# Two weight matrices converted where they are used, a scratch tile of its own for the conversion, and the sink rows of v loaded earlier, in an attention and feed-forward kernel on one core

## The chip, the cores and the metric

The kernel runs on one core of a Trainium2 chip. The metric is the time of one execution on the device, in microseconds (us); it is the median of the runs of one kernel. Engines are called as in the profile: PE multiplies matrices, PEld loads its weights, DVE is the vector engine, ACT the scalar engine, POOL is GpSimd, and SP issues DMAs.

## The reference

Sliding-window attention with sink keys for 4 batches, 8 heads, 768 rows and head size 64 (window 128, 4 sinks), then a feed-forward block with a squared ReLU (model 512, inner 2048), then a second block with two inputs multiplied (inner 1024) on the 3072 tokens of 512:

```python
attn = softmax(mask(q @ k.T / 8)) @ v            # per batch and head
x = attn.transpose(0, 2, 1, 3).reshape(3072, 512)
h = np.maximum(x @ w_in, 0.0)                    # w_in 512 x 2048
x = h * h @ w_out                                # w_out 2048 x 512
a, b = x @ w1, x @ w2                            # 512 x 1024 each
out = (a * b @ w3) @ w_out2                      # 1024 x 1024, 1024 x 512
```

The inputs of the attention and the weights lie in DRAM as float64.

## The kernel before

**Numbers.** Every matrix product of the two blocks is made of three f16 products: high by high, high by low, low by high. A weight is therefore prepared in two steps. First the float64 piece (128 x 512 numbers, 512 KB, in a tile named raw) becomes float32: `f64_to_f32_up` (L82 to L103) has ACT read the upper words as floats into cvy (L88), has DVE shift and mask the bits that are still missing in two instructions on 16-bit halves (L93, L96), and has DVE put both together (L99). `conv` (L1036) calls it. The two DVE shifts write over the raw tile itself, but for the pieces of `conv_late`, which take a scratch tile, cvt, of their own (`two=True`). Then `split` (L799) has ACT write the f16 high half and DVE (POOL for half of w_in) the low half. Raw pieces have two buffers (tag raw64). cvy and cvt are two of many names that share one ring of eight slots, tag t2 (`T2B = 8`): r, sq, x1e, the sink rows of v (vsr, vb, vt), and cp, cq, cr, asb of the output stage.

**Stages.** In the prologue the first 16 of 96 attention units are computed, and 8 pieces of w_in and some of the next are prepared. Six passes n = 0 to 5 over 512 tokens each follow, of 16 steps j (128 of the 2048 inner columns). One step is `ffn_A` (12 matmuls into hps), `ffn_act1` to `ffn_act3` (r, its square, and that as high and low half g), `ffn_B` of the step before (12 matmuls into x1ps), and, in passes 0 to 4, one attention unit of the tokens of the next pass (sc, softmax, pt, y). In passes 0 to 4 ACT, DVE and PE run in the order in which the program is written (the class `InOrder`, whose line L290 nearly every instruction bears); elsewhere a scheduler orders them. Pass 5 has no attention unit. The fold then makes w34 = w3 times w_out2: for each of eight f, `fold_T` transposes a row block of w3 on PE (w3ps, then w3T in two halves), and `fold_M` multiplies (24 matmuls into w34ps). The output stage takes six blocks of 512 tokens, each in eight f: `ffn_C` (a and b from w12, in seven products cps), `ffn_D` (ops) and `ffn_out`.

**Where weights are prepared.** The list `pieces` sets the order; `w_load` and `w_conv` walk it. w_in and w_out: prologue and pass 0. `load_late` and `conv_late` (L1076 to L1091): the 16 pieces of w3 and the 8 of w_out2 are converted in passes 1 to 3, one every two steps, and written back to DRAM as float32 (w3_dr, wo2_dr). w12 (16 pieces of w1 and w2, each pair summed as `ffn_C` needs it, `conv_w12` L1233): two late in pass 3, six in pass 4, six in pass 5, two in the fold. In pass 5 `load_wo2` (L1171) reads w_out2 back from DRAM and `split_wo2` has POOL make its low halves; `load_w3` (L1183) reads w3 back, one f at a time, for the fold.

**Sink rows of v.** Four times (b = 0 to 3), at unit ub - 1, `vs_load` (L621) clears a tile vsr on POOL and issues six small DMAs on SP, and `vs_make` at once works on it (vb, vt, vs on DVE). For b = 2 this is in pass 1, for b = 3 in pass 2; SP issues its DMAs in one order, the transposing loads of the probabilities (pt<-ph) among them.

## Time and profile before

| what | value |
|---|---|
| median of 3 runs | 1140.44 us (1139.66 to 1143.43) |
| the profiled execution, own time | 1145.11 us |
| its span in the trace | 1143.2 us |
| mean granted clock of PE | 0.973 of full speed |
| PE busy | 1051.2 us (92%) |
| DVE busy | 765.9 us (67%) |
| ACT busy | 703.2 us (62%) |
| POOL busy | 59.3 us (5%) |
| prologue | 0 to 91.2 us |
| passes 0 to 5 | from 91.2, 215.4, 322.3, 429.1, 536.5, 637.6 us |
| last hps ends, then fold | 726 us |
| output stage | 778.2 to 1143.2 us |

The starts of the passes are the first matmuls into hps of each. The busy share of the whole span says little, since the stages have different limits; what is read below is each stretch by itself. "Idle" of an engine is the time before an instruction in which it did nothing, with the event that ended it. A row of the chain of work that ended last names what was being waited for at that time, followed back from the end.

### The profile page before, as it was taken

How to read it: one execution, taken by the hardware profiler on the slowest of the kernel's cores; microseconds unless marked ns; L12 is line 12 of the kernel's file. 1: busy time of each engine (PE TensorE's matmuls, PEld its weight loads, DVE VectorE, ACT ScalarE, POOL GpSimd, SP SyncE). 2: the span in 40 equal slices, each digit the busy share in tenths (PEclk: the TensorE clock that was granted, in tenths of full speed). 3: DMA queues.
4: the chain of work that ended last, by engine and by line, in shares of the span. 5: the costliest groups of instructions: out<-in, count | busy, mean ns of one | idle time of the engine just before them, and what ended most of it. 6: DMA issues, size and time to landing. Idle time of an engine off the chain costs nothing.

```text
span 1143.2 us, 20444 instructions
## 1 busy us (share of the span) xinstructions
PE 1051.2 (92%) x7146; PEld 632.9 (55%) x7146; DVE 765.9 (67%) x2284; ACT 703.2 (62%) x1832; POOL 59.3 (5%) x167
## 2 busy tenths in 40 slices
PE   6777889999899989998999989999999999999996
PEld 5663444555455535544454434456767676767774
DVE  8997889877688868867997555555363636353433
ACT  6975768877467647655776785555464545464432
POOL 2111102000000000000000110000000000000000
PEclk9977989999899989999999999999999999999999
DMA  8847688989698868897853222123020101010101
GB/s 188 159 120 175 156 188 184 180 197 181 128 207 174 166 141 190 168 177 143 167 129 98 79 86 79 57 74 111 1 74 1 74 1 38 1 38 1 37 1 40
DMA packets 271232, 126.05 MB, mean 110 GB/s; under 512 B 238224, under 2 KB 254608, under 8 KB 270480
## 3 DMA queue, kind: packets, MB, share of 16 engines
q1 hardware_dynamic: 270832, 124.13, 48.7%
q8 instruction: 58, 0.95, 0.4%
q14 instruction: 54, 0.44, 0.1%
q10 hardware_dynamic: 288, 0.52, 0.1%
HBM read 68.37 MB, written 17.83 MB: 75 GB/s over the span
## 4 chain that ended last, share of the span: by engine, by line
PE 58%; DVE 16%; DMA 12%; ACT 7%; issue 3%; SPq 2%; POOL 0%; DVEq 0%; ACTq 0%
PE cps L290 18%; PE hps L290 12%; PE x1ps L290 11%; PE ops L290 11%; DMA pt<-ph 3%; PE w34ps L290 3%; DMA raw<-in_moe_w_dram 2%; DMA raw<-in_moe_w_out_dram 2%; PE y L290 2%; DVE pr L290 2%; DMA raw<-in_moe_w_in_dram 2%; DVE raw L96 2%; DVE cvy L99 2%; PE sc L290 2%; DVE raw L93 1%
## 5 line engine op out<-in xcount | busy, mean ns | idle before, releaser
L290 PE MATMUL x1ps<-g,wo 128*128 128x512 f16 x1152 | 271.9, 385 | 9.4 <-DVE g L290 6.9
L290 PE MATMUL hps<-xT,wi 128*128 128x512 f16 x1152 | 270.4, 385 | 2.8 <-ACT r L290 2.8
L290 PE MATMUL cps<-x1T,w 128*128 128x256 f16 x2016 | 231.5, 273 | 7.3 <-DVE cq L290 4.6
L290 PEld LDWEIGHTS <-w 128*128 128x128 f16 x2016 | 197.1, 98 | 44.4 <-issue 9.2
L290 PEld LDWEIGHTS <-wo 128*128 128x128 f16 x1152 | 111.2, 99 | 134.2 <-issue 20.3
L290 PEld LDWEIGHTS <-wi 128*128 128x128 f16 x1152 | 115.1, 100 | 125.5 <-issue 11.3
L290 PE MATMUL ops<-w,h 128*128 128x512 f16 x576 | 133.5, 379 | 1.8 <-ACT h L290 1.8
L290 ACT ACTIVATE r<-hps 128x512 f32<-128x512 f32 x96 | 56.8, 592 | 99.9 <-PE hps L290 97.5
L290 ACT ACTIVATE cp<-cps 128x256 f32<-128x256 f32 x96 | 36.1, 376 | 131.3 <-PE cps L290 131.3
L290 ACT ACTIVATE pr<-pr,stt 128x264 f32<-128x264 f32 (+1 forms) x176 | 77.5, 483 | 61.6 <-DVE stt L290 60.6
L290 PEld LDWEIGHTS <-h 128*128 128x128 f16 x576 | 56.3, 98 | 58.1 <-ACT h L290 2.1
L290 DVE SCALAR_TENSOR_TENSOR asb<-cq,cps 128x256 f32<-128x256 f32 x48 | 20.2, 420 | 87.6 <-PE cps L290 87.6
L290 DVE TENSOR_TENSOR ph<-pr,ph 128x512 f16<-128x512 f32 (+2 forms) x148 | 58.3, 431 | 30.6 <-ACT ph L290 30.6
L290 DVE CUSTOM_DVE_ANT_0 pr<-sc,mask 128x264 f32<-128x264 f32 (+1 forms) x176 | 65.4, 402 | 4.6 <-PE sc L290 4.3
L290 PEld LDWEIGHTS <-pt 128*128 128x128 f16 x956 | 40.0, 99 | 47.7 <-issue 24.6
L290 PE MATMUL y<-vp,pt 128*128 128x65 f16 (+1 forms) x888 | 41.1, 195 | 24.4 <-DVE xn L290 20.2
L290 PE MATMUL sc<-kT,qT 128*128 128x128 f16 x592 | 48.9, 223 | 13.1 <-DVE stt L290 13.0
L93 DVE TENSOR_SCALAR raw<-raw 128x512 uint16<-128x512 uint16 x48 | 36.7, 764 | 36.1 <-DMA raw<-in_moe_w_dram 23.0
L290 PEld LDWEIGHTS <-qT 128*128 128x128 f16 x592 | 41.3, 99 | 32.9 <-issue 9.8
L290 ACT ACTIVATE ph<-pr 128x512 f16<-128x512 f32 (+2 forms) x148 | 55.7, 420 | 5.1 <-DMA pt<-ph 3.1
L290 ACT ACTIVATE g<-r 128x512 f16<-128x512 f32 x88 | 55.3, 628 | 2.4
L88 ACT ACTIVATE cvy<-raw 128x512 f32<-128x512 f32 x72 | 48.1, 668 | 10.5 <-DMA raw<-in_moe_w_out_dram 9.3
(194 smaller groups left out, 1507.2 us busy)
## 6 DMA issues: line engine op xcount, KB each, us to landing
raw<-in_moe_w_dram SPq DMA_DIRECT2D x32, 512.0 KB
raw<-in_moe_w_out_dram SPq DMA_DIRECT2D x24, 512.0 KB
raw<-in_moe_w_in_dram SPq DMA_DIRECT2D x16, 512.0 KB
raw<-in_k_dram SPq DMA_DIRECT2D x84, 64.0 KB
raw<-in_q_dram SPq DMA_DIRECT2D x84, 64.0 KB
raw<-in_v_dram SPq DMA_DIRECT2D x84, 64.0 KB
x_dr<-x1e SPq DMA_DIRECT2D x20, 256.0 KB
x1s<-x_dr SPq DMA_DIRECT2D x5, 1024.0 KB
```

The source lines that it names most:

```text
L88: nc.scalar.activation(out=y.bitcast(F32), in_=raw.bitcast(F32)[:, :, 1], func=ACTF.Abs, scale=2.0 ** -111, accum_out=stat)
L93: nc.vector.tensor_scalar(out=t2[:, :, 0], in0=half[:, :, 1], scalar1=13, scalar2=None, op0=ALU.logical_shift_right)
L96: nc.vector.tensor_scalar(out=t2[:, :, 1], in0=half[:, :, 3], scalar1=0x8000, scalar2=None, op0=ALU.bitwise_and)
L99: nc.vector.scalar_tensor_tensor(out=dst, in0=y, scalar=3, in1=t, op0=ALU.logical_shift_left, op1=ALU.bitwise_or)
L290: r = f(*args, **kw)
```

## The change

- `f64_to_f32_up` always gets a scratch tile: `conv` takes cvt from the ring t2 for every piece, and the raw tile is only read.
- w3_dr, wo2_dr, `load_late` and `conv_late` are gone. The 8 pieces of w_out2 are converted in pass 5 and split at once (low halves on DVE, no longer on POOL); the pieces of w3 are loaded and converted in the fold, and `fold_T` transposes from the converted tile. Of w3, even f go into a 1 MB tile in the place of the output tile ost, odd f into the two raw buffers.
- Pass 5 has a list of 16 items, one a step: w_out2 four, w12 two, w_out2 two, w12 two, w_out2 two, w12 four; then the loads of w3 f = 1.
- w12: one pair of pieces in each of passes 1 to 4, at j = 4 and 5, with the loads of the next ones behind the conversions; 8 pieces in pass 5; none in the fold.
- vsr has a tile of its own in the attention's pool, and `vs_load` is called at unit ub - 6 for b = 1 to 3; `vs_make` stays at ub - 1.
- `ffn_out` is called after the second part of `ffn_C` rather than ahead of it.

```diff
...
 UP_MOST = 2.0 ** 31
 
 
-def f64_to_f32_up(nc, raw, y, dst, stat, t=None):
-
-
-    own = t is None
-    t = raw[:, :, 0] if own else t
+def f64_to_f32_up(nc, raw, y, dst, stat, t):
+
+
     nc.scalar.activation(
         out=y.bitcast(F32), in_=raw.bitcast(F32)[:, :, 1], func=ACTF.Abs, scale=2.0 ** -111, accum_out=stat
     )
     half = raw.bitcast(U16)
-    t2 = half if own else t.bitcast(U16).rearrange("p (n c) -> p n c", c=2)
+    t2 = t.bitcast(U16).rearrange("p (n c) -> p n c", c=2)
     nc.vector.tensor_scalar(
         out=t2[:, :, 0], in0=half[:, :, 1], scalar1=13, scalar2=None, op0=ALU.logical_shift_right
     )
...
 
     dram = ctx.enter_context(tc.tile_pool(name="dram", bufs=1, space=DRAM))
     x1_dr = dram.tile([NB, 128, KD, BT], F32, name="x1_dr")
-    w3_dr = dram.tile([K2, 128, DF2], F32, name="w3_dr")
-    wo2_dr = dram.tile([K2, 128, DM], F32, name="wo2_dr")
     xg_dr = dram.tile([NT, DM], F32, name="xg_dr")
     top = ctx.enter_context(tc.tile_pool(name="top", bufs=1))
     nsw = top.tile([128, 2], F32, name="nsw")
...
 
         def vs_load(b):
 
-            vsr = vsr_b[b] = slab("t2", [128, HP * D], F32, "vsr", bufs=T2B)
+            vsr = vsr_b[b] = att.tile([128, HP * D], F32, tag="vsr", name="vsr")
             POOL.memset(vsr, 0.0)
             for h in range(2):
                 for g in range(3):
...
             for b in range(B):
                 n = max(n for n in range(NK) if T0[n] <= b * TS)
                 ub = max(U0[n] + b * TS - T0[n], UB - 4)
-                if u == ub - 1:
+                if u == (ub - 6 if b else ub - 1):
                     vs_load(b)
                 if u == ub - 1:
                     vs_make(b)
...
             SP.dma_start(out=fl, in_=sb32)
             return raw
 
-        def conv(raw, dst=None, two=False):
+        def conv(raw, dst=None):
             if raw.dtype == F32:
                 ACT.activation(out=raw, in_=raw, func=ACTF.Copy, scale=W_UP)
                 return raw
             y = slab("t2", [128, 512], I32, "cvy", bufs=T2B)
             if dst is None:
                 dst = y.bitcast(F32)
-            t = slab("t2", [128, 512], I32, "cvt", bufs=T2B) if two else None
+            t = slab("t2", [128, 512], I32, "cvt", bufs=T2B)
             i = cvn[0]
             cvn[0] += 1
             f64_to_f32_up(nc, raw, y, dst.bitcast(I32), st_w[:, i:i + 1], t)
...
             x = conv(raw_w.pop(("wo", j)))
             w = wo_t[c]
             split(x, w[:, 0, j % 4, :], w[:, 1, j % 4, :], hi_eng=DVE if j < KF // 2 else ACT)
-
-        def load_late(i):
-
-            raw_w["late", i] = f32_piece(late_src(i))
-
-        def late_src(i):
-            if i < 2 * K2:
-                return w3[(i // 2) * 128:(i // 2 + 1) * 128, (i % 2) * 512:(i % 2 + 1) * 512]
-            return w_out2[(i - 2 * K2) * 128:(i - 2 * K2 + 1) * 128, :]
-
-        def conv_late(i):
-            x = conv(raw_w.pop(("late", i)), two=True)
-            if i < 2 * K2:
-                dst = w3_dr[i // 2, :, (i % 2) * 512:(i % 2 + 1) * 512]
-            else:
-                dst = wo2_dr[i - 2 * K2]
-            SP.dma_start(out=dst, in_=x)
 
         hps_t = {}
 
...
 
         wo2_t, w3s_t, w3T_t, w34_t = {}, {}, {}, {}
 
-        def load_wo2(c):
-            st = slab("raw64", [128, 2, DM], F32, "stg_wo2", bufs=2)
-            SP.dma_start(out=st, in_=wo2_dr[2 * c:2 * c + 2].rearrange("j p f -> p j f"))
-            w = late_p[0].tile([128, 2, 2, DM], F16, tag=f"wo2_{c}", name="wo2")
-            wo2_t[c] = (st, w)
-
-        def split_wo2(c):
-            st, w = wo2_t[c]
-            split(st, w[:, 0], w[:, 1], POOL)
-            upper(w[:, 0].rearrange("p j f -> p (j f)"))
-            wo2_t[c] = w
-
-        def load_w3(f):
-            st = slab("raw64", [128, K2, 128], F32, "stg_w3", bufs=2)
-            SP.dma_start(out=st, in_=w3_dr[f].rearrange("p (e c) -> p e c", c=128))
-            w3s_t[f] = st
+        def load_wo2(j):
+            raw_w["wo2", j] = f32_piece(w_out2[j * 128:(j + 1) * 128, :])
+
+        def conv_wo2(j):
+            c = j // 2
+            if c not in wo2_t:
+                wo2_t[c] = late_p[0].tile([128, 2, 2, DM], F16, tag=f"wo2_{c}", name="wo2")
+            w = wo2_t[c]
+            split(conv(raw_w.pop(("wo2", j))), w[:, 0, j % 2], w[:, 1, j % 2])
+            if j % 2:
+                upper(w[:, 0].rearrange("p j f -> p (j f)"))
+
+        def load_w3(f, m=None):
+
+            src = [w3[f * 128:(f + 1) * 128, c * 512:(c + 1) * 512] for c in range(2)]
+            if f % 2:
+                for c in range(2) if m is None else (m,):
+                    w3s_t.setdefault(f, []).append(f32_piece(src[c]))
+                return
+            both = late_p[0].tile([128, 2, 512, 2], I32, tag="ost", name="raw_w3")
+            for c in range(2):
+                if w3.dtype == F32:
+                    d = both[:, c].rearrange("p n c -> p (n c)")[:, 0:512].bitcast(F32)
+                    SP.dma_start(out=d, in_=src[c])
+                else:
+                    d = both[:, c]
+                    SP.dma_start(out=d.rearrange("p n c -> p (n c)"), in_=src[c].bitcast(I32))
+                w3s_t.setdefault(f, []).append(d)
 
         def fold_T(f):
-            st = w3s_t.pop(f)
+            st = [conv(r) for r in w3s_t.pop(f)]
             w = late_p[0].tile([128, 2, K2, 128], F16, tag="x1s", name="w3T", bufs=2)
             for g in range(2):
                 ps = bank(f"s{g}", "w3ps")
                 for e in range(4):
-                    PE.transpose(out=ps[:, e * 128:(e + 1) * 128], in_=st[:, g * 4 + e, :], identity=ident)
+                    PE.transpose(out=ps[:, e * 128:(e + 1) * 128], in_=st[g][:, e * 128:(e + 1) * 128], identity=ident)
                 split(
                     ps.rearrange("p (e c) -> p e c", c=128), w[:, 0, g * 4:g * 4 + 4, :],
                     w[:, 1, g * 4:g * 4 + 4, :],
...
             if u > TBF and (u - 1) % TBF == 0 and (u - 1) // TBF <= HP:
                 split_v(u - 2)
 
-        for i in range(3 * K2):
-            pieces.append((load_late, conv_late, i))
-        for i in range(2 * K2):
+        for i in range(K2):
             pieces.append((load_w12, conv_w12, i))
-        n0 = 2 * KF + 3 * K2
+
+        items = [(load_wo2, conv_wo2, i) for i in range(K2)]
+        for i in range(K2):
+            items.insert((4, 5, 8, 9, 12, 13, 14, 15)[i], (load_w12, conv_w12, K2 + i))
+        items += [(lambda i: load_w3(1, i), None, i) for i in range(2)]
+
+        def item_load(i):
+            items[i][0](items[i][2])
+
         pend = []
-        late, uo = [0], UB + LEAD
+        uo = UB + LEAD
         for s in range(NK * KF):
             n, j = divmod(s, KF)
             last = n == NK - 1
...
             if n == 0:
                 want = min(2 * KF, want0[j] + 1)
             elif not last:
-                late[0] += 1
-                want = 2 * KF + min(3 * K2 + K2, (late[0] + 1) // 2)
-            else:
-                want = n0 + K2 + max(0, 2 * (j // 4) - (j % 4 == 0))
-            while ncv[0] < want and ncv[0] < len(pieces):
+                want = 2 * KF + 2 * (n - 1) + (j >= 4) + (j >= 5)
+            if last:
+                if j == 0:
+                    item_load(0)
+                    item_load(1)
+                items[j][1](items[j][2])
+                item_load(j + 2)
+            while not last and ncv[0] < want and ncv[0] < len(pieces):
                 w_load(ncv[0] + 1)
                 w_conv()
-                if not last:
-                    w_load(min(ncv[0] + 2, n0 + K2))
+                w_load(ncv[0] + 2)
             ffn_act1(n, j)
             for u in us:
                 if ok(u):
...
                 if ok(u - 3):
                     att_X(u - 3)
             if last:
-                if j % 4 == 3 and j < 15 or j in (4, 8, 12):
-                    w_load(ncv[0] + 1)
+                if j == KF // 2:
+                    load_w3(0)
                 w = wi_t[j][:, 0] if j < KF // 2 else wo_t[(j - KF // 2) // 2][:, 0, j % 2 * 2:j % 2 * 2 + 2]
                 upper(w.rearrange("p c f -> p (c f)"))
-                if j in (0, 1, 5, 6):
-                    load_wo2((0, 1, 5, 6).index(j))
-                if j in (2, 3, 6, 7):
-                    split_wo2((2, 3, 6, 7).index(j))
-
         n = NB - 1
-        load_w3(0)
-        load_w3(1)
         for b in pend:
             ffn_B(*b)
         x1_last(n)
...
                 load_w3(f + 2)
             if f + 1 < K2:
                 fold_T(f + 1)
-            if f in (1, 2):
-                w_load(n0 + 14 + f)
-                w_conv()
             fold_M(f)
         x1_load(1)
         rest = [w[0][:, c:d].rearrange("p a c f -> p (a c f)") for w in w12_t.values() for c, d in ((0, 4), (4, 7))]
...
                 next(c)
                 if pend is not None:
                     ffn_D(*pend)
-                    if pend[1] == K2 - 1:
-                        ffn_out(pend[0], o - 1, False)
                 next(c)
+                if pend is not None and pend[1] == K2 - 1:
+                    ffn_out(pend[0], o - 1, False)
                 pend = (n, f)
                 if f < 4:
                     upper(x1_t[n][0][:, 2 * f:min(7, 2 * f + 2)].rearrange("p a c f -> p (a c f)"))
```

Engine DVE, the end of pass 5, before (st_g, sq and g belong to the steps 14 and 15; raw_9555 is a piece of w12; x1f, x1t, x1T are the result of pass 5):

```order
L290 TENSOR_TENSOR g<-r,g 128x512 [waits Activation_49]
L290 TENSOR_TENSOR w3T<-w3ps,w3T 128x512 [waits Activation_49] x2
L290 ISA sq,st_g<-r 128x512 [waits Activation_49]
L290 ISA st_g 128x1
L290 TENSOR_TENSOR g<-sq,g 128x512 [waits DVE_49,Activation_49]
L93 TENSOR_SCALAR raw_9555<-raw_9555 128x512 [waits DMAHW4_49,DMAHW6_49,DMAHW2_49,PE_49]
L96 TENSOR_SCALAR raw_9555<-raw_9555 128x512 [waits DVE_49]
L99 SCALAR_TENSOR_TENSOR cvy<-cvy,raw_9555 128x512 [waits DVE_49,Activation_49]
L290 TENSOR_TENSOR g<-r,g 128x512 [waits Activation_49]
L290 TENSOR_TENSOR w_9616<-cvy,w_9615 128x512 [waits PE_49,Activation_49]
L290 TENSOR_SCALAR x1f_9444<-x1ps 128x512 [waits PE_49]
```

The same place after (w_9322 is w12, raw_w_9015 the even f = 0 of w3, raw_9279 and raw_9334 the pieces of f = 1, raw_w_9425 those of f = 2):

```order
L91 TENSOR_SCALAR cvt<-raw_w_9015 128x512
L94 TENSOR_SCALAR cvt<-raw_w_9015 128x512
L91 TENSOR_SCALAR cvt<-raw_w_9015 128x512
L94 TENSOR_SCALAR cvt<-raw_w_9015 128x512
L91 TENSOR_SCALAR cvt<-raw_9279 128x512 [waits DMAHW2_49,DVE_49]
L94 TENSOR_SCALAR cvt<-raw_9279 128x512
L288 TENSOR_TENSOR w_9322<-w12s,w_9321 128x1024 [waits Activation_49]
L97 SCALAR_TENSOR_TENSOR cvy<-cvy,cvt 128x512 [waits DVE_49,Activation_49] x3
L91 TENSOR_SCALAR cvt<-raw_9334 128x512 [waits DMAHW3_49,DVE_49]
L94 TENSOR_SCALAR cvt<-raw_9334 128x512
L288 TENSOR_TENSOR g<-r,g 128x512 [waits Activation_49]
L91 TENSOR_SCALAR cvt<-raw_w_9425 128x512 [waits DMAHW4_49,PE_49]
```

Ahead of the last g<-r of the pass stand eight shifts and three L97 of w3 and the split of a w12 pair; before, one w12 piece stood there, and w3T of an earlier f.

Queue of SP, the loads of the sink rows for b = 2, before, in pass 1 (raw with a number are weight pieces, raw without are q, k, v; w_dr are converted pieces going back to DRAM):

```order
L1091 DMA w_dr<-cvy 128x512
L1033 DMA raw_3883<-in_moe_w_dram 128x1024
L742 DMA_TRANSPOSE pt<-ph_104 128x9x128
L559 DMA_TRANSPOSE kT<-pkk 128x4x128 x2
L628 DMA vsr<-in_v_dram 8x4x64 x3
L742 DMA_TRANSPOSE pt<-ph_103 128x9x128
L628 DMA vsr<-in_v_dram 8x4x64 x3
L598 DMA_TRANSPOSE qT<-pkq 128x4x128
L1033 DMA raw_4092<-in_moe_w_dram 128x1024
L1091 DMA w_dr<-cvy 128x512
```

The loads for the same b after, at the start of pass 0:

```order
L555 DMA_TRANSPOSE kT<-pkk 128x4x128
L1029 DMA raw_1317<-in_moe_w_out_dram 128x1024
L624 DMA vsr<-in_v_dram 8x4x64 x2
L555 DMA_TRANSPOSE kT<-pkk 128x4x128
L594 DMA_TRANSPOSE qT<-pkq 128x4x128
L1029 DMA raw_1327<-in_moe_w_in_dram 128x4x256
L624 DMA vsr<-in_v_dram 8x4x64
L738 DMA_TRANSPOSE pt<-ph_101 128x9x128
L624 DMA vsr<-in_v_dram 8x4x64 x2
L738 DMA_TRANSPOSE pt<-ph_102 128x9x128
L738 DMA_TRANSPOSE pt<-ph_101 128x4x128
L624 DMA vsr<-in_v_dram 8x4x64
```

The six loads stood on both sides of one pt transpose at the unit that uses them. They now stand where their tile has become free after b = 1, at the start of pass 0; those for b = 3, which stood in pass 2, stand in pass 1.

## Rows read from the trace of the kernel before

**Rows 1.** Length; busy us (x) of PE, PEld, DVE, ACT, POOL; PEclk; DMA; GB/s
```profile
0.00:91.20 91.20, 65.94 (x420) 54.28 (x421) 79.47 (x353) 69.63 (x251) 17.19 (x49) 0.87 0.73 154
91.20:215.40 124.20, 104.25 (x686) 52.81 (x685) 109.31 (x326) 91.58 (x269) 14.47 (x31) 0.93 0.82 180
215.40:429.10 213.70, 202.13 (x1427) 105.34 (x1425) 164.61 (x569) 143.34 (x384) 8.87 (x48) 0.97 0.83 170
429.10:536.50 107.40, 99.82 (x699) 51.74 (x697) 82.87 (x281) 67.67 (x176) 6.85 (x27) 0.98 0.89 169
536.50:637.60 101.10, 97.04 (x679) 50.51 (x677) 82.96 (x266) 66.27 (x164) 2.98 (x10) 1.00 0.57 125
637.60:726.00 88.40, 84.03 (x400) 39.33 (x399) 47.21 (x77) 60.60 (x119) 8.93 (x4) 1.00 0.27 90
726.00:778.20 52.20, 50.90 (x255) 25.48 (x254) 28.44 (x47) 28.70 (x54) 0.00 (x0) 1.00 0.20 71
```

**Rows 2.** Timeline of PE, end of pass 0: start, us, operation
```profile
209.20 2.75 PE L290 MATMUL hps<-xT,wi 128*128 128x512 f16 x12
...
215.37 0.81 PE L290 MATMUL hps<-xT,wi 128*128 128x512 f16 x3
```

**Rows 3.** Chain of work that ended last, in pass 5: start, us, what
```profile
699.77 2.59 PE hps L290 x12
702.36 2.59 PE x1ps L290 x12
```

**Rows 4.** Groups, DVE, whole span: xcount | busy us, mean ns | idle
```profile
L93 DVE TENSOR_SCALAR raw<-raw 128x512 uint16<-128x512 uint16 x48 | 36.7, 764 | 36.1 <-DMA raw<-in_moe_w_dram 23.0 <-DMA raw<-in_moe_w_out_dram 11.3 <-DMA raw<-in_moe_w_in_dram 1.8
L96 DVE TENSOR_SCALAR raw<-raw 128x512 uint16<-128x512 uint16 x48 | 35.5, 740 | 0.3
...
L99 DVE SCALAR_TENSOR_TENSOR cvy<-cvy,cvt 128x512 int32<-128x512 int32 x24 | 16.6, 690 | 1.9 <-ACT cvy L88 1.8
...
L93 DVE TENSOR_SCALAR cvt<-raw 128x512 uint16<-128x512 uint16 x24 | 10.9, 455 | 0.0
L96 DVE TENSOR_SCALAR cvt<-raw 128x512 uint16<-128x512 uint16 x24 | 10.8, 450 | 0.0
```

**Rows 5.** The first shift in place, in the prologue and in pass 0
```profile
L93 DVE TENSOR_SCALAR raw<-raw 128x512 uint16<-128x512 uint16 x11 | 8.2, 745 | 1.7 <-DMA raw<-in_moe_w_in_dram 1.3 <-DMA raw<-in_moe_w_out_dram 0.3
...
L93 DVE TENSOR_SCALAR raw<-raw 128x512 uint16<-128x512 uint16 x21 | 15.7, 746 | 11.4 <-DMA raw<-in_moe_w_out_dram 10.9 <-DMA raw<-in_moe_w_in_dram 0.5
```

**Rows 6.** DVE's waits in passes 0 to 3: us in total, times, longest
```profile
DVE raw L93 <- DMA raw<-in_moe_w_out_dram: 10.9, 10, 2.4
...
DVE vb L290 <- DMA vsr<-in_v_dram: 7.7, 1, 7.7
...
DVE vb L290 <- DMA vsr<-in_v_dram: 8.2, 1, 8.2
...
DVE raw L93 <- DMA raw<-in_moe_w_dram: 7.7, 2, 5.1
```

**Rows 7.** Groups, DVE, whole span: split and sums of w12
```profile
L290 DVE TENSOR_TENSOR w<-w12s,w 128x1024 f16<-128x1024 f32 x8 | 9.8, 1228 | 2.2 <-ACT w L290 2.2
...
L290 DVE TENSOR_TENSOR w12s<-cvy 128x256 f32<-128x256 f32 x16 | 6.4, 421 | 0.1
```

**Rows 8.** Groups, ACT, whole span: first conversion step; split of staged w_out2
```profile
L88 ACT ACTIVATE cvy<-raw 128x512 f32<-128x512 f32 x72 | 48.1, 668 | 10.5 <-DMA raw<-in_moe_w_out_dram 9.3 <-DMA raw<-in_moe_w_in_dram 0.7 <-DMA raw<-in_moe_w_dram 0.5
...
L290 ACT ACTIVATE wo<-stg_wo 128x1024 f16<-128x1024 f32 x4 | 4.1, 1048 | 4.6 <-DMA stg_wo<-wo_dr 4.6
```

**Rows 9.** Groups, POOL, whole span: low half of w_in
```profile
L805 POOL TENSOR_TENSOR wi<-cvy,wi 128x512 f16<-128x512 f32 x8 | 11.6, 1447 | 41.4 <-ACT wi L290 41.4
```

**Rows 10.** Chain of work that ended last, end of pass 5 and fold
```profile
728.72 4.10 PE w34ps L290 x19
...
752.43 6.48 PE w34ps L290 x30
...
773.25 4.86 DMA x1s<-x_dr
```

## The prediction

> **What bounds the kernel now.** I read first the busy times by stretch. The stretches are the prologue, the passes of w_in and w_out (pass 0, passes 1 and 2 together, 3, 4, 5), and the fold that makes w34 [rows 1]; the output stage after them is left alone by this change, because every engine has the same instructions in the same order there. In each stretch compare PE's busy time with the length: passes 4, 5 and the fold are PE's (97.0 of 101.1, 84.0 of 88.4, 50.9 of 52.2), passes 1 to 3 nearly so, but pass 0 leaves PE 20 us idle and the prologue 25 us. In both DVE is the fullest engine (109.3 of 124.2; 79.5 of 91.2).
>
> Second, what a step costs when nothing holds PE. Two neighbouring steps of pass 0 start 6.17 us apart at its end [rows 2]: 24 matmuls of the FFN and one attention unit. In pass 5, without attention, hps and x1ps follow each other without a gap at 2.59 us each, 5.18 a step [rows 3]. So a pass of 16 attention steps has a floor of 16 x 6.17 = 98.7. In pass 4 units run out: twelve full steps and four between 5.18 and 6.17, for which I take 5.5, give 96. Above these floors lie 124.2 - 98.7 = 25.5 in pass 0, 213.7 - 197.4 = 16.3 in passes 1 and 2, 107.4 - 98.7 = 8.7 in pass 3, and 5.1 in pass 4. That is what there is to win before the fold.
>
> Third, what held DVE in those stretches [rows 6]. In pass 1 it stood 7.7 us for the sink rows of v and in pass 2 8.2, which PE then lacks: together 15.9, nearly all of the 16.3. In pass 3 it stood 7.7 us, in two waits, for raw w12, nearly all of the 8.7. In pass 0 it waited ten times for raw w_out, 10.9 us in all.
>
> **The change part by part.**
> *Own scratch for the conversion.* The two shifts of one conversion take 0.76 and 0.74 when they write into the raw tile, and 0.455 and 0.450 when they write into a tile of their own [rows 4]: 0.60 us saved each time, the same instruction and shape. The prologue has 11 in-place conversions, pass 0 has 21 [rows 5]. The prologue's 11 x 0.6 = 6.6 us of DVE lie in an engine 87% busy, but not all on the path; a third may hide, and ring slots taken by the scratch may hold others back. I take **-4** (bounds -9, if what frees up lets the next load start sooner, and +2).
> In pass 0, 21 x 0.6 = 12.6 us leave DVE. It was 88% busy, so if all else scales the pass shrinks by 12.6 / 0.88 = 14.3. The raw tile also comes free one instruction earlier, since the third one (0.69 [rows 4]) now reads the scratch, and that pulls the next load forward and cuts the 10.9 us of waits. Against it: these waits are for 512 KB loads in SP's single order, and may stay. I take **-13**, nearer to full scaling because DVE is the fullest engine; bounds -5 (waits stay whole and the freed time falls among them) and -20 (4/5 of the 25.5 above the floor).
> First, the in-place and own-tile rows differ by 0.60 us for one conversion [rows 4]. The Trainium skill, "VectorE: DVE Perf Modes", section "What auto-detection actually checks", makes the double rate hang on a single source and destination in SBUF with even or equal outermost dims, which holds for both forms; by it the two would cost alike and this part of the sum would be nothing. The trace disagrees (0.764 against 0.455), and the measurement decides; the rule is rival 2.
>
> *w3 and w_out2 leave passes 1 to 3.* 24 conversions go: of DVE 24 x (0.455 + 0.450 + 0.69) = 38 us [rows 4], of ACT 24 x 0.67 = 16 us [rows 8], and the write to DRAM of 256 KB behind each. Both engines had room there (DVE 164.6 of 213.7), PE sets the pace, so this gains only what it spares in stalls.
> *Sink rows of v.* Their loads and memset move at least five units ahead, at 6.17 us a unit 31 us, in a tile of their own. On SP's queue they stand further ahead still, those of pass 1 at the start of pass 0 and those of pass 2 in pass 1, spread among the pt transposes (the order shows it). Both waits vanish; at the new places a pt transpose has one or two of six short issues ahead of it, and the tile was given up by DVE before that unit's own work, so I put them at nothing. What is late next is PE itself.
> *w12.* Two pieces in each of passes 1 to 4, at steps 4 and 5, loaded a pass ahead, in place of eight in passes 3 and 4 with their late loads. So pass 3's 7.7 us go. What comes new is a pair in two steps: besides two conversions, four sums of 0.42 and the split of 1.23 and smaller ones [rows 7], some 7 us of DVE more over two steps, while DVE (about 82 us busy of 107 with 7 or 8 conversions, some 70 without) has about 2 us of slack a step. A pair can thus cost 0 to 4; I take 2, times four passes, +8.
> Passes 1 to 4 together: lost above floor 16.3 + 8.7 + 5.1 = 30; less 8 for the pairs, and 1 left of odd waits: **-21** (bounds -26 and -13).
>
> *Pass 5 and fold.* Pass 5 gets the eight w_out2 pieces and eight of w12, one a step. ACT: 8 conversions and 8 splits of about 0.67 [rows 8] are 10.7, less four splits of 1.05 that go, plus two more w12 pieces, about 3: 60.6 becomes some 70 of 88.4, with DVE's at 47 + 8 x 2.3 = 65. PE stays the bound but g can now come late at times; **+4** (0 to 10). POOL's four splits go, which nobody waited for.
> At the end of pass 5 the order of after puts between hps of step 15 and the low half of its g a run of DVE work that stood elsewhere: by the rows of like shape 0.69 + 0.42 + 6 x 0.45 + 1.23 + 3 x 0.69 + 2 x 0.45 + 0.69 = 8.7 us [rows 4, 7]. PE has x1ps of step 14 (2.59) and one f's transposes (about 0.9) for it. The cover of before is gone: there 19 matmuls of w34ps, 4.10 us, ran just ahead of the last x1ps [rows 10]. So PE stands 0 to 5.2 us; **+5**, the far end, as all those instructions hang on loads and on ACT.
> In the fold one f costs PE 24 matmuls at 0.216 (6.48 us for 30 [rows 10]) = 5.2, and 0.87 of transposes: 6.1. DVE gets two conversions of 1.6 per f on top of the two halves of w3T: 28.4 + 7 x 3.2 - 2 of w12 (about 9) = 42 of 52.2. PE stays the bound, if barely. Loads of w3 are 1 MB per f; 1 MB took 4.86 us at the fold's end [rows 10], under 6.1, with two f in flight: hidden, 5 us once if the cover fails. Pass 5 and fold: **+9** (+2 to +20).
>
> *Moved output rows' emission.* The order on all engines is the same: 0.
>
> Sum: -4 - 13 - 21 + 9 = -29 on the profiled execution of 1145.1 us (span 1143.2): 1116. That execution lay 4.7 us above the median of 1140.44 that a result is set against, so the same step from there gives **1111**.
>
> **The rivals.**
> 1. *Pass 0 stays behind its loads.* DVE's 10.9 us of waits for w_out [rows 6] are ten loads in SP's order; if the load and not DVE sets the pace, faster shifts only lengthen the waits. For it: DMA share 0.82 there. Against: DVE 88% busy. Pass 0 gives 2 to 3 rather than 13: 1122. Chance 12%.
> 2. *In-place was as fast as own tile.* The 0.60 would then come from the place, not the form (in-place rows from the busy prologue and pass 0, own-tile rows from quieter passes). Against: medians alike in every stretch (745, 746 [rows 5]). The first two terms vanish: 1128. 4%.
> 3. *The fold runs in lock-step: slower.* Conversions, cvy and cvt of w3 all take slots of one ring of eight, and transposes wait for them. If an f goes through one after the other (ACT, two shifts, third, transposes, two splits: 0.45 + 0.45 + 0.69 + 0.5 + 0.6 + 0.7 = 3.4 a half, 6.7 an f, then 5.2 of matmuls and 1 of hand-offs) it costs 13 rather than 6.1: 8 x 7 = 55 in place of the 5: about 1160. It decides from 6.1 + 34 / 8 = 10.3 us an f, where the other terms are eaten up. For it: DVE and ACT must keep an f ahead on one ring. Against: two loads and two w3T tiles are there, and PE has 24 matmuls of cover. 6%.
> 4. *The w12 pairs cost 5 each*, as 7 us of DVE land ahead of a unit's exponentials: 20 instead of 8: 1123. 9%.
> 5. *Pass 0 falls to its floor:* -25 and the prologue with it -6: 1097. 9%.
> 6. *POOL and DVE shut each other out.* POOL's eight splits of w_in, 1.45 us each [rows 9], run in the prologue and pass 0 beside the conversions. If each held up a faster shift whole, 8 x 1.45 = 11.6 come back: 1123. 2%, since in-place shifts beside it keep a median of 745 [rows 5]. The Trainium skill, "SBUF — State Buffer", section "Who interferes with whom", has it that a DVE instruction in a two-port mode and a GpSimd one exclude each other for a whole instruction; no row of before shows an own-tile shift beside such a split.
>
> **How the numbers follow.** My forecast, as summed, has 58%. Its own range is 1100 to 1121. To hold 8 in 10 the range takes in rivals 1, 4, 5, 6 and most of 2, and leaves out 3: **1096 to 1130**. About 0.3%, 3.4 us, is what a measurement of this kernel can tell from no change. Slower by more is rival 3 (6%); within it, a partial rival 3 or a sum of 1, 2 and 4 (3%); faster, the rest (91%).
>
> **What would show it.** In the profile of after: all shifts on DVE near 0.45; pass 0 about 111 long and DVE's waits for w_out not above 11; no wait for the sink rows of v and passes 1 to 3 near 101 each, with the pairs at steps 4 and 5 the only long steps; pass 5 about 92, with a gap of up to 5 on PE ahead of the last x1ps, and then 6.1 an f. Wrong would be: a fold of over 70 us (rival 3), pass 0 above 118 with longer load waits (1), shifts near 0.74 (2), shifts of 1.5 beside POOL (6), steps 4 to 6 over 8 us (4). If the output stage moved by more than 2 us, the reading of the order was wrong.

## The result and the profile after

The changed kernel takes 1110.24 us (median of 4 runs, 1107.25 to 1110.35) where the kernel before takes 1140.15 (now of four runs): the ratio is 0.9725, with a 95% interval of 0.9701 to 0.975. Its profiled execution took 1110.19 us (span 1108.0). The forecast was 1111. That it came within 1 us is luck: two of the sum's four terms lay outside their bounds, and the errors cancelled each other.

The stretches after, as [rows 1] has them before (length; busy us and instructions of PE, PEld, DVE, ACT, POOL; granted clock of PE; DMA share; GB/s): prologue, pass 0, passes 1 to 4, pass 5, fold. The last two are cut at the end of the last hps and at the first cps; before, that end lay at 726.1, so that pass 5 was 88.5 and the fold 52.1.

```profile
0.00:94.56 94.56, 69.36 (x420) 59.22 (x421) 77.25 (x358) 70.64 (x253) 14.86 (x50) 0.81 0.79 166
94.56:211.88 117.32, 102.99 (x686) 52.45 (x685) 98.21 (x318) 91.47 (x266) 11.40 (x31) 0.94 0.79 176
211.88:600.52 388.64, 388.64 (x2800) 206.54 (x2798) 303.33 (x1049) 266.44 (x674) 18.72 (x84) 1.00 0.62 126
600.52:683.60 83.08, 81.03 (x374) 36.40 (x373) 54.98 (x112) 64.39 (x137) 0.00 (x0) 1.00 0.36 119
683.60:743.60 60.00, 56.15 (x281) 28.70 (x279) 45.69 (x89) 41.12 (x88) 0.00 (x0) 0.97 0.36 124
```

| stretch | before | after | difference | forecast (bounds) |
|---|---|---|---|---|
| prologue | 91.2 | 94.6 | +3.4 | -4 (-9 to +2) |
| pass 0 | 124.2 | 117.3 | -6.9 | -13 (-20 to -5) |
| passes 1 to 4 | 422.2 | 388.6 | -33.6 | -21 (-26 to -13) |
| pass 5 and fold | 140.6 | 143.1 | +2.5 | +9 (+2 to +20) |
| output stage | 365.0 | 364.4 | -0.6 | 0 |
| span | 1143.2 | 1108.0 | -35.2 | -29 |

In passes 1 to 4 PE is now busy in all of the 388.64 us: no wait of PE is left there. Before, it was busy 398.99 of 422.20 us with the same matmuls. So 23.2 of the 33.6 us that went were idle time, and 10.4 were matmuls that took longer, at a mean granted clock of 0.98 rather than 1.00. One place shows how: in pass 1 of before DVE waits for the sink rows until 293.76, PE stands about 5 us for DVE's work behind that wait (stt), and then the mean granted clock is 0.54 (298.36 to 303.40 us; near the lower of its two levels, 1.2 GHz). Eleven matmuls take 4.35 us there, where twelve take 2.75 elsewhere (timeline of PE, before; in brackets the idle time before and what ended it):

```profile
297.85 0.72 PE L290 MATMUL sc<-kT,qT 128*128 128x128 f16 x4 [4.95 <-DVE stt L290]
...
299.29 4.35 PE L290 MATMUL x1ps<-g,wo 128*128 128x512 f16 x11 [0.29 <-DVE g L290]
```

After, the steps around j = 4 and 5 of pass 1, where a pair of w12 pieces is prepared, start 6.17 us apart, like those of [rows 2] (timeline of PE: start, length):

```profile
236.56 2.75 PE L288 MATMUL hps<-xT,wi 128*128 128x512 f16 x12
...
242.74 2.75 PE L288 MATMUL hps<-xT,wi 128*128 128x512 f16 x12
...
248.91 2.75 PE L288 MATMUL hps<-xT,wi 128*128 128x512 f16 x12
```

The shifts all have the short form, as against [rows 4] (groups of DVE, whole span; the pieces of w3 with even f, 8 more of each, have means of 470 and 468 ns):

```profile
L91 DVE TENSOR_SCALAR cvt<-raw 128x512 uint16<-128x512 uint16 x64 | 29.3, 457 | 15.3 <-DMA raw<-in_moe_w_out_dram 10.5 <-DMA raw<-in_moe_w_in_dram 4.7
L94 DVE TENSOR_SCALAR cvt<-raw 128x512 uint16<-128x512 uint16 x64 | 28.8, 450 | 0.0
```

In pass 0 the waits of [rows 6] for raw w_out are hardly smaller, 9.8 us against 10.9, and PE still waits for DVE (waits of DVE and of PE in pass 0: us in total, times, longest):

```profile
DVE cvt L91 <- DMA raw<-in_moe_w_out_dram: 9.8, 5, 2.9
...
PE y L288 <- DVE xn L288: 13.4, 5, 3.6
```

At the end of pass 5 PE stands 2.38 us for the conversion of the first w3 piece (the chain of before had 4.10 us of w34ps there [rows 10]). Later in the fold an f takes 6.05 us, from 714.65 to 720.70 (timeline of PE):

```profile
683.50 2.75 PE L288 MATMUL x1ps<-g,wo 128*128 128x512 f16 x12
688.63 0.63 PE L288 MATMUL w3ps<-ident,cvy 128*128 128x128 f32 x4 [2.38 <-DVE cvy L97]
...
714.65 0.60 PE L288 MATMUL w3ps<-ident,cvy 128*128 128x128 f32 x4
...
717.67 0.60 PE L288 MATMUL w3ps<-ident,cvy 128*128 128x128 f32 x4
...
720.70 0.60 PE L288 MATMUL w3ps<-ident,cvy 128*128 128x128 f32 x4
```

### The profile page after: what moved, and what is told of

It is laid out like the page before. It is cut to its first block, busy times and chain, and to the rows that moved or that the text cites. A ratio compares the mean times of both kernels' runs of the same rounds, so it can differ in the third digit from the quotient of the medians.

```text
span 1108.0 us, 20449 instructions
## 1 busy us (share of the span) xinstructions
PE 1045.3 (94%) x7146; PEld 636.4 (57%) x7146; DVE 750.3 (68%) x2292; ACT 709.4 (64%) x1836; POOL 45.0 (4%) x163
## 5 line engine op out<-in xcount | busy, mean ns | idle before, releaser
L288 PE MATMUL x1ps<-g,wo 128*128 128x512 f16 x1152 | 265.6, 380 | 3.0 <-ACT g L288 2.0
L288 DVE TENSOR_TENSOR ph<-pr,ph 128x512 f16<-128x512 f32 (+2 forms) x148 | 59.2, 436 | 35.2 <-ACT ph L288 33.2
L288 DVE TENSOR_TENSOR g<-r,g 128x512 f16<-128x512 f32 x56 | 38.6, 689 | 24.6 <-ACT g L288 24.4
L97 DVE SCALAR_TENSOR_TENSOR cvy<-cvy,cvt 128x512 int32<-128x512 int32 x72 | 49.1, 688 | 8.5 <-ACT cvy L86 8.3
L288 DVE TENSOR_TENSOR h<-asb,h 128x512 f16<-128x512 f32 x48 | 33.2, 691 | 28.2 <-ACT h L288 28.2
```

Of the source, the lines that this page charges most:

```text
L97: nc.vector.scalar_tensor_tensor(out=dst, in0=y, scalar=3, in1=t, op0=ALU.logical_shift_left, op1=ALU.bitwise_or)
L288: r = f(*args, **kw)
```

## The experiments

Each is a short edit to the kernel before or to the changed one. Times are medians. Where a ratio is given, it is to the kernel before, run beside it on the same chip; on the chips used here that kernel had medians of 1140.15 to 1144.76 us, so times of different experiments can be set against each other to a few us only.

**The kernel before once more.** No edit.

> The kernel before, unchanged, for a second trace of it: its profiled execution lay about 5 us above the median of its runs. If those 5 us were in the stretches that wait for loads (prologue and pass 0, 215.4 us together in the first trace), this trace reaches pass 1 after some 210 to 212 us, with the later passes as long as before. If they were in passes 1 to 4, these sum to some 417 instead of 422.2 us. Time 1140 either way.

1144.22 us, span 1142.4: prologue 91.9, pass 0 123.7, passes 1 to 4 421.6, pass 5 and fold 140.6. The stretches of the first trace repeat within 1.5 us, so that differences of 3 us and more between traces of these stretches can be read. (The output stage, the same instructions in all kernels, is 364 to 369 us long in the traces.) The profiled executions of this kernel are 5.0 and 1.8 us above its medians, and the difference is in neither of the two places where it was looked for.

**The scratch tile alone.** Before, with

```diff
-            t = slab("t2", [128, 512], I32, "cvt", bufs=T2B) if two else None
+            t = slab("t2", [128, 512], I32, "cvt", bufs=T2B)
```

> The kernel before with a scratch tile of its own for every conversion, and nothing else of the change. Theory of the prediction (DVE sets the pace of prologue and pass 0): 17 us less there, and 2 or 3 in passes 3 and 4: about 1121. Rival (raw loads set the pace, which the trace of after speaks for: prologue and pass 0 together were only 3.5 us shorter): 2 to 5 us less, 1136, with DVE's waits for raw w_in and w_out grown by about what the shifts save.

1125.21 us, ratio 0.9857 (0.9821 to 0.9894). By size this is the forecast's theory; by place it is not. The prologue is 0.9 shorter, pass 0 10.0 (first row; [rows 1] has 124.20), but passes 1 to 4 together 11.7, above all pass 3 (second row, 107.40 before), where DVE no longer waits for raw w12. The output stage of this trace is 4.3 longer.

```profile
90.26:204.50 114.24, 101.38 (x685) 51.95 (x684) 98.64 (x321) 91.16 (x267) 14.00 (x31) 0.95 0.81 178
416.00:516.50 100.50, 97.70 (x698) 51.43 (x696) 82.07 (x279) 67.88 (x175) 4.59 (x27) 1.00 0.92 178
```

What became of the wait in pass 3 can be read from the traces. Before, the load of the first w12 piece is issued at 508.18, DVE stands at its first shift until 513.46, and the third instruction of the piece comes only 21 us later, at 534.64 (timeline of DVE, before):

```profile
513.46 0.73 DVE L93 TENSOR_SCALAR raw<-raw 128x512 uint16<-128x512 uint16 x1 [5.12 <-DMA raw<-in_moe_w_dram]
```

With the scratch, the load of that piece is issued at 495.94, its shift runs at 512.74 without a wait, and the third instruction follows at 514.42. So DVE was held there by the place of the shift, and not by a load that came too late for its use. Two experiments below, the shifts in place and the scratch outside the ring, show what sets this place.

**The sink rows alone.** Before, with

```diff
-            vsr = vsr_b[b] = slab("t2", [128, HP * D], F32, "vsr", bufs=T2B)
+            vsr = vsr_b[b] = att.tile([128, HP * D], F32, tag="vsr", name="vsr")
...
-                if u == ub - 1:
+                if u == (ub - 6 if b else ub - 1):
                     vs_load(b)
```

> The kernel before with the sink rows of v in a tile of their own and loaded at unit ub - 6, and nothing else of the change. Theory: the two waits of 7.7 and 8.2 us go, and nothing takes their place: about 16 us less, 1124. Rival: the float32 pieces on their way back to DRAM and the raw loads of w3 that are still in the same queue hold up something else at that place: 5 us less or fewer, 1135.

1130.03 us, ratio 0.9886 (0.9852 to 0.9921), some 13 us. Passes 1 and 2 are 200.85 long where [rows 1] has 213.70, and no wait for the sink rows is left in them:

```profile
216.65:417.50 200.85, 196.37 (x1427) 104.06 (x1425) 164.26 (x568) 143.28 (x382) 8.74 (x47) 1.00 0.89 180
```

**The shifts in place again.** After, with `t = None` in `conv` and the lines of before in `f64_to_f32_up`:

```diff
-    t2 = t.bitcast(U16).rearrange("p (n c) -> p n c", c=2)
+    own = t is None
+    t = raw[:, :, 0] if own else t
+    t2 = half if own else t.bitcast(U16).rearrange("p (n c) -> p n c", c=2)
```

> The changed kernel with the two shifts writing over the raw tile again, all else as changed. Theory of the prediction: prologue and pass 0 grow by 17 us, and pass 5 and fold by a few (0.6 us more for each of 32 conversions there, 19 us of DVE, on an engine with some room): 1127 to 1133. Rival (loads set the pace of pass 0): prologue and pass 0 grow by about 4, pass 5 and fold by up to 6: 1114 to 1120.

1169.37 us, ratio 1.0233 (1.02 to 1.0265): 59 us more than the changed kernel, which neither theory had. Pass 0 takes 9 more, pass 5 8, the fold 6, and passes 1 to 4 36.7 (stretches pass 0, passes 1 to 4, fold):

```profile
94.23:220.60 126.37, 103.47 (x686) 52.36 (x685) 111.44 (x328) 92.06 (x269) 15.11 (x31) 0.95 0.74 168
220.60:645.90 425.30, 398.35 (x2800) 209.74 (x2798) 306.99 (x1047) 268.44 (x674) 18.96 (x84) 0.98 0.55 115
737.00:802.90 65.90, 56.74 (x282) 28.77 (x280) 50.01 (x83) 40.89 (x87) 0.00 (x0) 0.97 0.36 120
```

The loss of passes 1 to 4 sits at the w12 pairs: steps 4 to 6 of pass 1 take 9.8, 13.7 and 7.1 us. There DVE stands 6.07 us for a raw piece whose load had just been issued, and PE then waits for xn of the attention, which stands behind that shift on DVE (timeline of DVE; waits of PE in passes 1 to 4):

```profile
253.24 0.74 DVE L93 TENSOR_SCALAR raw<-raw 128x512 uint16<-128x512 uint16 x1 [6.07 <-DMA raw<-in_moe_w_dram]
...
PE y L290 <- DVE xn L290: 21.5, 7, 6.1
```

The order shows why. Engine DVE in pass 1, in place (raw_3287 is a piece of the next pass's pair; its third instruction comes only in pass 2):

```order
L93 TENSOR_SCALAR raw_3287<-raw_3287 128x512 [waits DMAHW4_49]
L290 TENSOR_TENSOR xn<-y,den_3268 128x128 [waits DVE_49]
```

The conversion's instructions are not kept in program order. In place the shift needs no slot of the ring, and it stands right behind its load, a pass early, and ahead of xn: its load is issued at 248.91 and it runs at 253.24. With cvt in the ring of eight, the load of the same piece is issued at 237.50 and the shift runs at 330.47, in pass 2, long after the load has landed. That it is the slots of the ring which hold it there is what the next experiment tests.

**The scratch outside the ring.** After, with

```diff
-            t = slab("t2", [128, 512], I32, "cvt", bufs=T2B)
+            t = slab("cvt", [128, 512], I32, "cvt", bufs=2)
```

> The changed kernel with the scratch in two buffers of its own, out of the ring of eight slots that it shares with r, sq, cvy and the rest. If the scratch, by taking ring slots, is what made the prologue 3.4 us longer, prologue and pass 0 together shrink by 4 to 10 us: 1100 to 1106. If the ring was never full, the time stays: 1109 to 1112.

1139.03 us (10 runs, 1134.88 to 1143.51), ratio 0.9974 (0.9952 to 0.9995): 28 us slower than with the ring, by the ratios. The shifts are as short as in the changed kernel; again it is passes 1 to 4, 419.7 us, with the first steps of a pair at 7.7, 12.9 and 7.9 in pass 1, and DVE's waits in these passes have (us in total, times, longest):

```profile
DVE cvt L91 <- DMA raw<-in_moe_w_dram: 14.1, 5, 4.5
```

The shifts run ahead again: the load that follows the first conversion of pass 1 is issued at 236.18, DVE stands at its shift until 240.48, with xn behind it, and the third instruction of that piece comes at 339.70, in pass 2. PE waits seven times for xn in these passes, 19.2 us (timeline of DVE):

```profile
240.48 0.45 DVE L91 TENSOR_SCALAR cvt<-raw 128x512 uint16<-128x512 uint16 x1 [4.55 <-DMA raw<-in_moe_w_dram]
240.83 0.28 DVE L288 TENSOR_TENSOR xn<-y,den 128x128 f32<-128x128 f32 x1
```

So not the scratch tile as such but its slots in the ring keep the shifts from running ahead.

**Slow shifts in a scratch tile.** After, with a scratch of [128, 512, 2] in one buffer, of which every second word is used, so that the 16-bit elements that a shift writes lie 8 bytes apart, as in the raw tile.

> The changed kernel with one scratch tile whose 16-bit halves lie 8 bytes apart, as in the raw tile, instead of 4. It tells what made a shift in place take 0.75 us and one into a scratch 0.45: if it is writing over the tile that is read, these shifts take 0.45 us; if it is the distance of the elements written, 0.75. As there is one buffer, conversions may wait for each other; time 1110 to 1130.

1115.57 us (one run, span 1113.3), within what was expected. The shifts are slow again without being in place (groups of DVE, whole span):

```profile
L95 DVE TENSOR_SCALAR cvt<-raw 128x512 uint16<-128x512 uint16 x64 | 50.4, 788 | 0.0
L92 DVE TENSOR_SCALAR cvt<-raw 128x512 uint16<-128x512 uint16 x64 | 48.0, 750 | 9.0 <-DMA raw<-in_moe_w_out_dram 8.0 <-DMA raw<-in_moe_w_in_dram 0.4
```

And yet pass 0 is as long as in the changed kernel, 117.50 against 117.32, with 6.8 us more of DVE's busy time in it, and passes 1 to 4 too; only the fold grows by 4.8 (stretches pass 0, passes 1 to 4, fold):

```profile
94.46:211.96 117.50, 101.53 (x685) 51.84 (x684) 104.97 (x320) 91.28 (x266) 18.37 (x31) 0.95 0.79 179
211.96:600.76 388.80, 388.79 (x2800) 206.80 (x2798) 306.89 (x1048) 266.11 (x674) 17.86 (x84) 1.00 0.61 125
683.00:747.80 64.80, 57.16 (x281) 28.67 (x279) 53.93 (x87) 41.32 (x87) 0.00 (x0) 0.95 0.34 114
```

So the short form of the shifts is worth up to 5 us in the fold, the single buffer's part in that included. In pass 0 it is worth little: nothing beside the changed kernel, and 3.7 us beside the kernel with fast shifts off the ring, whose pass 0 took 113.8. Off the ring too, DVE waits for no w12 piece here. One shift of each pair still runs a pass early (at 242.96 in pass 1, its third instruction at 332.42), but with a single buffer it has to stand behind the third instruction of the piece before (241.41), and by then its load, issued at 237.89, has landed.

**Three raw buffers.** After, with

```diff
-            raw = slab("raw64", [128, 512, 2], I32, "raw64", bufs=2)
+            raw = slab("raw64", [128, 512, 2], I32, "raw64", bufs=3)
```

> The changed kernel with three buffers for the raw pieces instead of two. If raw loads of w_in and w_out set the pace of pass 0 because they must wait for a buffer, DVE's waits of 9.8 us for raw w_out shrink and pass 0 (117.3 us, 18.6 above 16 steps of 6.17) shrinks by 5 to 15 us: 1096 to 1105. If they wait for their turn in SP's queue or DVE sets the pace, it stays within 3 us: 1108 to 1113.

1093.63 us, ratio 0.958 (0.9545 to 0.9615): the fastest kernel of this study. The edit pays in one place: pass 0 takes 103.2 us rather than 117.3 (from the first hps at 92.4 to 195.6; the prologue 92.4), the rest is as long as in the changed kernel. The waits for raw w_out, 9.8 us in pass 0 and 10.5 in all, are down to 1.7 in the whole span. (Row of pass 0; group of DVE.)

```profile
92.40:195.60 103.20, 97.49 (x687) 51.12 (x685) 96.57 (x321) 91.49 (x269) 14.62 (x31) 0.98 0.95 199
...
L91 DVE TENSOR_SCALAR cvt<-raw 128x512 uint16<-128x512 uint16 x64 | 30.1, 470 | 3.3 <-DMA raw<-in_moe_w_out_dram 1.7 <-DMA raw<-in_moe_w_in_dram 1.5
```

So what pass 0 waits for are raw loads, and these wait for a buffer.

**Three raw buffers before the change.** The same edit to the kernel before (with the staged w_out2 and w3, which share that tag).

> The kernel before with three buffers for raw pieces instead of two (shifts still in place), nothing of the change. Theory (a raw load can only be issued once a buffer is free, and it is that which pass 0 and the late loads of w12 wait for): pass 0 shrinks by 8 us, passes 3 and 4 by some 5 to 10, the two waits for sink rows stay: 1122 to 1130. Rival (with shifts in place they only move further ahead behind their loads, and DVE waits all the same): 1136 to 1145.

1149.97 us, ratio 1.007 (1.0042 to 1.0099): a little slower, so that the rival had the mechanism, though the time lies above its range too. Pass 0 gains 7 us, to 117.1, but DVE still stands 28.3 us for raw pieces in the span, 18.5 of them of w12 (the pieces of w3 go through cvt; groups of DVE; waits of PE in pass 0), the prologue is 3.6 us longer, and pass 5 (91.1), fold and output stage some 7. The w12 shifts do move further ahead: the first one now stands 33 us ahead of its third instruction (497.90 and 531.06), before 21.

```profile
L93 DVE TENSOR_SCALAR raw<-raw 128x512 uint16<-128x512 uint16 x48 | 37.4, 780 | 28.3 <-DMA raw<-in_moe_w_dram 18.5 <-DMA raw<-in_moe_w_out_dram 6.8 <-DMA raw<-in_moe_w_in_dram 2.7
...
PE y L290 <- DVE xn L290: 12.8, 7, 4.0
```

**The order kept.** Two kernels record the four instructions of the conversion through the class that keeps program order in passes 0 to 4: the in-place one, and the one with three raw buffers.

```diff
-            f64_to_f32_up(nc, raw, y, dst.bitcast(I32), st_w[:, i:i + 1], t)
+            f64_to_f32_up((ACT, DVE), raw, y, dst.bitcast(I32), st_w[:, i:i + 1], t)
```

> The changed kernel with the shifts in place again, and with the conversion's four instructions recorded through the class that keeps program order in passes 0 to 4, as all other work there. In the in-place kernel without this, passes 1 to 4 took 425.3 us against 388.6. Theory (without a slot of the ring the shifts are free to be moved ahead, right behind their load, and DVE waits there): with the order kept, passes 1 to 4 come back to 389 to 396 us, pass 0 to 117 to 126, the fold stays near 65: 1118 to 1132. Rival (the longer hold on the raw tile or DVE's time is what costs): passes 1 to 4 stay near 425: 1160 to 1170.

1185.89 us, ratio 1.0362 (1.033 to 1.0393). Neither is right. Passes 1 to 4 recover 15 of the 36.7 us (410.5), and no wait of DVE for a w12 piece is left in them; but a pair in place and in order still costs some 5 to 7 us (steps 5 and 6: 9.2 and 7.9 in pass 1, 10.7 and 8.9 in pass 4). That is another wait, and the order brings it: r, which hps waits for, now stands on ACT behind the conversion and split of the pair, and PE stands four times for it, 13.5 us in all. So this run does not tell how much of the 36.7 us the running ahead alone was. Pass 0 grows to 158.6 in the same way (waits of PE in pass 0):

```profile
PE hps L290 <- ACT r L290: 42.6, 11, 6.5
```

> The changed kernel with three raw buffers, as in the run that took 1093.6, and the conversion kept in program order in passes 0 to 4. If the ring had already held the shifts at their places, nothing moves: 1092 to 1096. If the scheduler had been moving conversions of pass 0 ahead to good effect, pass 0 grows by 3 to 8 us: 1096 to 1102; if it had moved them to ill effect, it shrinks by as much: 1086 to 1091.

1140.6 us (10 runs), ratio 0.9959 (0.9939 to 0.9978): some 45 us slower than the same kernel with a free order, far from all three ranges. Pass 0 takes 141.2, with 28.2 us of PE waiting for r. Step 5 of passes 1 to 4 takes 7.8, 7.5, 8.5 and 8.2 instead of 6.2: in program order a pair costs 1.3 to 2.3 us, and where the scheduler moves its instructions, nothing.

**The sink rows in the changed kernel.** First the call alone at its old place, then the ring of before as well:

```diff
-                if u == (ub - 6 if b else ub - 1):
+                if u == ub - 1:
```

> The changed kernel with the sink rows of v loaded at unit ub - 1 again, at the place of their use, in their own tile. Theory (the place in SP's queue makes the wait): 7 to 8 us of waiting come back in pass 1 and as much in pass 2: about 1126. Rival (the wait came from the raw loads and the write-backs of w3 in the same queue, which are gone): 0 to 4 us come back: 1110 to 1114.

1109.2 us, ratio 0.9719 (0.9684 to 0.9754): as the changed kernel. The loads stand at the same places of SP's queue, because they are not kept in program order either, and their own tile is free early.

> The changed kernel with the sink rows' tile back in the ring of eight slots and its loads called at unit ub - 1, as before the change. With the call alone moved back and the tile kept apart the loads stood at the same places of SP's queue and nothing changed. Theory (a slot of the ring becomes free only shortly before its use, so its loads cannot be issued earlier): waits of 7 to 8 us come back in pass 1 and in pass 2: 1122 to 1127. Rival (the waits came of the traffic for w3 in the same queue, which is gone): 1109 to 1114.

1108.4 us, ratio 0.9682 (0.9654 to 0.9709): no slower. The loads move back to their use, and DVE waits 8.8 us for them in passes 1 and 2, half of the 15.9 of [rows 6]; but PE, which lost 13 us to that before, loses 1.1 in waits, and the two passes are 2.6 longer (waits of DVE and PE in passes 1 and 2):

```profile
DVE vb L288 <- DMA vsr<-in_v_dram: 8.8, 2, 4.8
...
PE x1ps L288 <- DVE g L288: 0.6, 2, 0.3
PE sc L288 <- DVE stt L288: 0.5, 1, 0.5
```

The early loads of the sink rows are worth 13 us in the kernel before and at most 3 in the changed one: this edit and the rest of the change win the same time. That it is the 24 conversions gone from passes 1 to 3 which give DVE the room to catch up is likely, but not shown: no run moves w3 and w_out2 alone, nor the w12 pairs alone.

## Why the forecast was right, and where it was not

*Which stretches gain.* Right: passes 1 to 4 give nearly everything, the output stage nothing, pass 5 and the fold together lose a little. No rival decided the time. The lengths named as signs were mostly missed: pass 0 is 117.3 (about 111 forecast), passes 1 to 3 are 98.3, 97.2 and 97.2 (near 101), pass 5 is 83.1 (about 92).

*Prologue, -4.* Wrong in sign: +3.4. With the scratch alone it is 0.9 shorter; in the kernels built on the change it is 90.3 to 95.6 long. PE's idle time is the same, 25.2 us (25.3 before): faster shifts took nothing from it, and DVE waits 4.7 us for raw w_in (1.3 before). What grew is the time of the same 420 matmuls, 69.4 us rather than 65.9, at a granted clock of 0.81 (0.87 before). Which part of the change does it was not settled.

*Pass 0, -13.* It was mis-sized (-6.9; -10.0 with the scratch alone, and what the rest of the change costs there is open) and, worse, explained by the wrong step, "if all else scales the pass shrinks by 12.6 / 0.88". The pass did not scale with DVE's time: slow shifts in a scratch tile cost pass 0 between nothing and 3.7 us where the scaling gives 14. The rest of what is gained comes of the separate tile. Whether by the earlier release of the raw buffer, or by the other order that the scheduler makes of it, was not told apart; the waits for w_out, 10.4 us in place and 9.8 in scratch, hardly differ. Rival 1 had the true limit of this pass, its loads, though they did not wait longer, as it had it. A third raw buffer takes 14 of the 18.6 us that stand above 16 steps of 6.17. A busy share of 88% was read as "this engine sets the pace"; 10.9 us of waits in ten places beside it were the better sign.

*Passes 1 to 4, -21.* Mis-sized by 12.6, nearly all in two terms. The pairs were priced at 8 and cost 0; the price of 2 a pair is what program order would have cost (1.3 to 2.3), but the scheduler moved the shifts between other work. And the floor of 98.7 was 1.5 too high in passes 2 and 3, where every second step takes 5.9 to 6.0, for 3.4 in all; the last 1 is the odd waits, which are gone too. What vanished is otherwise as listed, all of the 30 us above the floors. But that pass 3's wait came of late loads was wrong: the shift stood too early, and the scratch alone removed the wait. And part of what the waits cost was clock, for which the working had no term: 10.4 of the 33.6 us. Rival 4 (pairs of 5 and more) did come in the in-place kernel and in the one with the scratch off the ring: how near it lay could not be seen from the profile, as it hangs on which instructions may be moved, not on DVE's slack.

*Sink rows.* The two waits were right for the kernel before (13 us measured alone, where 16 were counted). That DVE's 7.7 us in pass 1 equal what the step lost (13.9 rather than 6.2) is in part chance: PE stood idle 5.2 us of it, and the rest is matmuls at the lower clock. That the two waits add to the gain of the other edits was not so.

*Pass 5 and fold, +9.* +2.5, made of -5.4 in pass 5 and +7.9 in the fold; 24 transposes of w3 and 2 matmuls of w34ps that ran in pass 5 before now run behind it, which the working did not have. The stall ahead of the last x1ps was there, at 2.4 rather than 5.2, and it was the transposes of w3 ahead of it that waited. The +4 for late g's was not: the steps of pass 5 take 5.2 as before, and PE's idle time there is 2.05 us (4.4 before). An f takes 6.05, as worked out (6.1): rival 3's lock-step did not come.

*Shifts beside POOL (rival 6).* It did not come, but was hardly tried: after, only one shift overlaps a split of w_in in time, at 0.445 us. With the scratch alone three do, and one of them took 0.917 us.

*In place or not (rival 2).* The difference between 0.76 and 0.45 is real, but it comes neither of the place nor of the tile being read: a scratch tile with the elements 8 bytes apart has it too. The rule of the Trainium skill that was weighed ("VectorE: DVE Perf Modes", section "What auto-detection actually checks") names where source and destination lie and their dimensions, and not this distance; the trace disagrees with it as far as it would make all three forms alike (0.76, 0.46 and 0.75 us for the first shift).

*The step to the median.* The profiled execution before lay 4.7 us over the median that the forecast starts from, and that after on its own (1110.19 against 1110.24). So the sum missed the traces by 6 us (-29 against -34.9) and the medians by 1 (-29 against -29.9): the two traces are further apart than the medians, and that hid what was left of the errors.

## What to carry to other kernels

A scratch tile does more than hold data: the ring that it is taken from decides how far ahead the scheduler may move its instruction, and where an instruction was moved right behind its load, DVE stood, with work behind it that was ready: 31 us here for four pairs of pieces, when the same scratch left the ring. Price a wait of PE with the clock in it: in passes 1 to 4 of before the lower clock came to 10.4 us on top of 23.2 of idle time. Before pricing an engine's time at a high busy share, ask whether waits stand beside it: with 10 us of waits for loads in a pass, one more buffer gave 14 us and faster instructions 4 at most. (The buffer alone, without the scratch from the ring, made the kernel before 0.7% slower.) Gains of two edits that fill the same slack (an earlier load, and less work on the engine that waits for it) do not add.

## What the runs showed of the hardware

A DVE shift of 128 x 512 16-bit elements that are read 8 bytes apart takes 0.74 to 0.79 us on average when it writes them 8 bytes apart, and 0.45 to 0.46 us when it writes them 4 bytes apart, in whatever tile (in place 0.764 and 0.740, in a scratch at 8 bytes 0.750 and 0.788, in one at 4 bytes 0.457 and 0.450).

Here a wait of PE cost more than its length. Behind 4.95 us of idle time in pass 1 of before the mean granted clock was 0.54 from 298.36 to 303.40 us, and 11 matmuls took 4.35 us; from 303.40 to 306 it was 1.00 again.
